# Attention in front of a routed mixture of experts: scores computed once per head in a corner of the array, the second softmax turned by VectorE

## The chip, the core and the metric

The kernel runs on one core of a Trainium2 chip. A core has TensorE (PE, matmuls from SBUF into the eight PSUM banks), VectorE (DVE), ScalarE (ACT), GpSimd (POOL, which does not read PSUM here) and SyncE (SP, which starts DMAs). Each engine works through its own queue in order and waits on semaphores for the others. The metric is the time of one execution on the device in microseconds; everything is float32.

## The reference

Eight batches of eight heads; a head has 512 tokens `x` and 32 state rows, each of 64 values. Tokens read the state and the state reads the tokens, from the same products with two different softmaxes; then every one of the 8 x 544 rows (512 values, all heads side by side) goes through one of eight experts.

```python
scores  = scale * x @ state.T                      # (B, H, 512, 32)
a       = softmax(scores);  xread = a @ state      # (B, H, 512, 64)
scores2 = scale * state @ x.T                      # (B, H, 32, 512): scores, transposed
a2      = softmax(scores2); sread = a2 @ x         # (B, H, 32, 64)
x       = concatenate([xread, sread], tokens)      # rows of H * D = 512 values
logits  = x @ w_gate;  local = sigmoid(x @ w_local)
# in token order: e = argmax(logits) where it is the first token or local < 0.5, else the e before
out     = softmax(logits)[e] * (relu(x @ w1[e]) @ w2[e])
```

## The kernel before

The program has three stages: `attention`, then `Routing.route`, then `experts`. The instructions of each engine are put in order by a scheduler of the framework, which places them by its own estimate, so the order in the code and that in the queues differ. Tiles rotate through pools; a tile of a pool with n buffers waits until the tile n before it has been read. All of PSUM is one pool of eight single banks (`bank()`).

**Attention** loops over the eight batches. `load` brings `x` twice: `x_t`, transposed (pairs of heads on 128 partitions, 512 tokens along them), and `x_n`, tokens on partitions; three buffers of each. At the start the state is laid out with zeros around it: `std` (its transpose, four heads on the diagonal of blocks, so that one 128x128 tile of weights serves two heads and two heads' rows are zero) and `sd` (the state itself, four heads a group on a block diagonal). `sw` is the product of the state with the gate weights (L121), so that a token's gate logits come from its softmax weights too.

For each of the two groups of four heads, `weights` computes the scores twice: `s2`, (head, state) on partitions over 512 tokens (L138), and `s1`, tokens on partitions over (head, state) (L144). From `s2` come the state's weights `e2` (max L148, Exp L152 with its sum, scaling L161), from `s1` the tokens' weights `e1` (max over 32 L155, subtraction L157, Exp L158, sum L163, multiplication on POOL L166). `turned` turns both by PE against an identity (L173, L178), with copies out of PSUM on ACT (L175) and DVE (L180). `read` multiplies: the state's reading `rps` (L188, copied to `rt` on DVE, L194), the tokens' values `v` (L201, copied to `xr` on ACT, L207), the tokens' logits (L204), and for the 32 state rows a transpose and their logits (L214, L217). Then the gate's softmax, and rows of 520 values (512 and 8 probabilities) go to `rows` in DRAM. The softmaxes of batch b + 1 are written ahead of `read` of batch b.

**Routing** starts with L288 on all tokens' logits: a chain of small DVE operations, transposes and matmuls that gives each token a slot, sorted by expert in blocks of 128. **Experts** runs 41 blocks, each with a gather of 128 rows (POOL), 4 MB of weights (SP), 4 transposes, 32 matmuls of 128 columns (L437), 8 of 512 (L442), and a scatter.

## Time and profile before

| what | value |
|---|---|
| runs (median of 3; lowest to highest) | 876.18 us; 876.18 to 879.81 |
| profiled execution, first to last instruction | 877.5 us (no other time is given for it) |
| PE busy, weight loads busy | 795.2 us (91%), 600.2 us (68%) |
| DVE, ACT, POOL busy | 182.8 us (21%), 111.1 us (13%), 103.5 us (12%) |
| attention, to the start of L288 | 179.9 us |
| routing, from L288 to the first gather | 179.9 to 216.9 us |
| experts | 216.9 us to the end |

The profiled execution's span lies among the runs' times, 1.3 us above their median. A line of the chain of waits reads: start in us, length in us, engine, tile, line of the kernel, number of records. A line of the groups reads: line, engine, operation, out<-in, shapes, count, then busy us and mean ns of one, then the engine's idle time before them and what ended it. A line of the stretches reads: from:to, length, then busy us (and count) of PE, of its weight loads, of DVE, ACT and POOL, then the granted clock of PE, the share of the DMA engines and GB/s.

### The profile page before, as it was taken

The page shows a single profiled execution, that of the slowest core. Times are in us where ns is not written, and L with a number is a line of the kernel's source. Part 1 is how long each engine was busy: PE and PEld are TensorE (multiplying, and loading weights), DVE is VectorE, ACT ScalarE, POOL GpSimd, SP SyncE. Part 2 cuts the span into 40 slices and gives each one's busy share as a digit, 9 for nine tenths or more (in the row PEclk, how much of TensorE's full clock was granted, in tenths as well). Part 3 has the DMA queues.
Part 4 walks back from the last instruction along what each step waited for, and adds up shares of the span by engine and source line. Part 5 has one row for each costly group of instructions (what it writes and reads, how often), then busy time and mean ns, then how long its engine had stood idle before and what let it go on. Part 6 is the DMA issues. An engine that isn't in the chain of part 4 may idle for free.

```text
span 877.5 us, 11051 instructions
## 1 busy us (share of the span) xinstructions
PE 795.2 (91%) x4658; PEld 600.2 (68%) x4658; DVE 182.8 (21%) x525; ACT 111.1 (13%) x200; POOL 103.5 (12%) x110
## 2 busy tenths in 40 slices
PE   6899999937899999999999999999999999999995
PEld 6588888927676666766757667576676766767663
DVE  2465555465100101001010010100101001001010
ACT  0333343310000010000100001000010000100000
POOL 2001110000110101101011010110100101001000
PEclk9799999965899999999999999999999999999998
DMA  8145531228488878888788788887888877788730
GB/s 335 49 148 177 198 118 55 102 87 354 155 318 301 297 286 304 321 297 300 277 306 317 292 296 292 307 316 281 297 298 303 316 287 290 292 307 308 271 144 1
DMA packets 25761, 219.41 MB, mean 250 GB/s; under 512 B 3760, under 2 KB 3760, under 8 KB 13168
## 3 DMA queue, kind: packets, MB, share of 16 engines
q1 hardware_dynamic: 14400, 189.29, 58.6%
q0 software_dynamic: 6560, 19.84, 6.0%
q10 hardware_dynamic: 4752, 9.58, 3.0%
q8 instruction: 37, 0.61, 0.3%
q14 instruction: 12, 0.10, 0.0%
HBM read 200.73 MB, written 19.80 MB: 251 GB/s over the span
## 4 chain that ended last, share of the span: by engine, by line
issue 65%; PE 21%; POOL 6%; DMA 4%; DVE 3%; POOLq 0%; SPq 0%; DVEq 0%
POOL out_dram L445 4%; PE ps L138 4%; PE ps L201 3%; PE ps L144 3%; PE ps L188 3%; DMA out_dram<-y,sidx 3%; PE ps L386 2%; POOL xg L401 2%; PE ps L121 2%; PE ps L204 1%; PE ps L178 1%; PE ps L173 1%; DMA sttc<-in_stt_dram 1%; DMA xg<-rows,gidx 0%; PE ps L214 0%
## 5 line engine op out<-in xcount | busy, mean ns | idle before, releaser
L437 PE MATMUL ps<-x_t,a 128*128 128x128 f32 x2624 | 305.9, 278 | 41.0 <-DVE x_t L430 41.0
L437 PEld LDWEIGHTS ps<-x_t,a 128*128 128x128 f32 x2624 | 298.1, 193 | 50.9 <-DVE x_t L430 50.9
L442 PE MATMUL ps<-c,h 128*128 128x512 f32 x656 | 288.3, 592 | 0.0
L442 PEld LDWEIGHTS ps<-c,h 128*128 128x128 f32 x656 | 121.5, 190 | 137.3 <-issue 137.3
L439 ACT ACTIVATE h<-ps 128x512 f32<-128x512 f32 x82 | 49.0, 597 | 632.5 <-PE ps L437 632.5
L401 POOL DMA_INDIRECT xg<-rows,gidx x41 | 40.0, 975 | 553.9 <-PE ps L428 500.0
L444 DVE TENSOR_SCALAR y<-ps,p 128x512 f32<-128x512 f32 x41 | 30.8, 751 | 284.6 <-PE ps L442 284.6
L423 DVE TENSOR_TENSOR own<-xg,ohb 128x8 f32<-128x8 f32 x41 | 6.9, 167 | 300.8 <-DMA xg<-rows,gidx 300.8
L445 POOL DMA_INDIRECT out_dram<-y,sidx x41 | 41.6, 1015 | 69.3 <-DVE y L444 58.0
L144 PEld LDWEIGHTS ps<-std,x_t 128*128 128x128 f32 x256 | 32.2, 197 | 8.8 <-issue 8.8
L428 PEld LDWEIGHTS ps<-ident,xg 128*128 128x128 f32 x164 | 20.7, 143 | 25.5 <-issue 25.5
L201 PE MATMUL ps<-sd,a 128*128 128x256 f32 x128 | 35.3, 398 | 0.0
L138 PE MATMUL ps<-x_t,std 128*128 128x512 f32 x64 | 33.7, 653 | 0.0
L166 POOL TENSOR_TENSOR e<-e,z 128x512 f32<-128x512 f32 x16 | 16.7, 1047 | 142.6 <-DVE z L160 109.6
L144 PE MATMUL ps<-std,x_t 128*128 128x128 f32 x256 | 32.0, 279 | 0.0
L188 PE MATMUL ps<-e,x_n 128*128 128x64 f32 x256 | 29.5, 273 | 0.0
L188 PEld LDWEIGHTS ps<-e,x_n 128*128 128x128 f32 x256 | 29.2, 192 | 0.0
L428 PE MATMUL ps<-ident,xg 128*128 128x128 f32 x164 | 25.1, 276 | 4.3 <-DMA xg<-rows,gidx 4.3
L430 DVE COPY x_t<-ps 128x512 f32<-128x512 f32 x41 | 27.9, 682 | 0.9 <-PE ps L428 0.9
L386 PE MATMUL ps<-bc,pc 128*128 128x41 f32 x80 | 17.3, 415 | 9.9 <-DVE bc L381 9.9
L386 PEld LDWEIGHTS ps<-bc,pc 128*128 128x128 f32 x80 | 17.1, 332 | 10.8 <-issue 10.8
L207 ACT COPY xr<-ps 128x512 f32<-128x512 f32 x32 | 18.8, 586 | 36.6 <-PE ps L201 36.6
(124 smaller groups left out, 343.1 us busy)
## 6 DMA issues: line engine op xcount, KB each, us to landing
a<-in_w_dram SPq DMA_DIRECT2D x41, 2048.0 KB, 7.8
c<-in_w_dram SPq DMA_DIRECT2D x41, 2048.0 KB, 8.9
rows<-xr ACTq DMA_DIRECT2D x8, 1040.0 KB, 4.3
x_t<-in_xt_dram SPq DMA_DIRECT2D x8, 1024.0 KB, 4.8
x_n<-in_xn_dram SPq DMA_DIRECT2D x8, 1024.0 KB, 5.4
xg<-rows,gidx POOLq DMA_INDIRECT x41, 8.4
out_dram<-y,sidx POOLq DMA_INDIRECT x41, 7.6
rows<-xs ACTq DMA_DIRECT2D x8, 65.0 KB, 4.0
```

Source lines behind the costliest of these rows:

```text
L138: nc.tensor.matmul(s2, lhsT=std[:, b, k, :], rhs=x_t[:, k, :], start=(k == 2 * g), stop=(k == 2 * g + 1))
L144: nc.tensor.matmul(s1[:, c * P:c * P + P], lhsT=x_t[:, k, c * P:c * P + P], rhs=std[:, b, k, :], start=(k == 2 * g), stop=(k == 2 * g + 1))
L188: nc.tensor.matmul(rps[:, k, :], lhsT=x_n[:, c, 2 * k:2 * k + 2, :].rearrange("p h d -> p (h d)"), rhs=e_t[k // 2][:, c, 64 * (k % 2):64 * ...
L201: nc.tensor.matmul(v[:, g * GD:g * GD + GD], lhsT=a_t[g][:, c * P:c * P + P], rhs=sd[:, b, g, :], start=True, stop=True)
L386: nc.tensor.matmul(who, lhsT=pc, rhs=bc[:, c], start=(c == 0), stop=(c == COLS - 1))
L401: nc.gpsimd.indirect_dma_start(out=xg, out_offset=None, in_=rows[:, :], in_offset=bass.IndirectOffsetOnAxis(ap=gidx[:, k:k + 1], axis=0))
L428: nc.tensor.transpose(tps[:, j * P:j * P + P], xg[:, j * P:j * P + P], ident)
L437: nc.tensor.matmul(hps[:, i * P:i * P + P], lhsT=a[:, j, m * P:m * P + P], rhs=x_t[:, j, :], start=(j == 0), stop=(j == KT - 1))
L439: nc.scalar.activation(h[:, half * 4:half * 4 + 4, :].rearrange("p m t -> p (m t)"), hps, Act.Relu)
L442: nc.tensor.matmul(yps, lhsT=h[:, m, :], rhs=c[:, m, :], start=(m == 0), stop=(m == FK - 1))
L444: nc.vector.tensor_scalar(y, yps, p, None, Alu.mult)
L445: nc.gpsimd.indirect_dma_start(out=out, out_offset=bass.IndirectOffsetOnAxis(ap=sidx[:, k:k + 1], axis=0), in_=y, in_offset=None, bounds_c ...
```

## The change

The scores are computed once. `scores` gives one head 64 rows and 32 columns of the array: pair k of heads goes to partitions 32k of the output, head u of the pair to bank u of a tile `s` of two banks (one buffer). All eight heads of a batch are one tile of 128 partitions and 2 x 512 columns. `softmaxes` then handles a batch at once, in operations of 1024 columns instead of two of 512: the state's weights `e2` from `s`, and the tokens' weights from `s` after DVE has transposed it in blocks of 32x32, so that 32 states lie along a row; POOL now subtracts the max as well as multiplying by the reciprocal, and a second 32x32 transposition by DVE makes `a`, the form that the products take. `turned` keeps the PE transposes of `e2` alone. The state with its gate logits is one tile `sd` of 256 + 9 columns a group; its logits come from `gates` in corners of the array too, and the separate logits product (L204) is gone: they come out of the value product and are added from its two groups by DVE. `std` and its layout are gone; `sd` is filled by POOL. PSUM in the attention is split: two single banks, two for `s`, two buffers of two banks for `v`; routing and experts have eight banks again. Rows get 530 values, their head order and that of `w1` differ to suit. The reductions, experts and routing are otherwise as they were, with later line numbers.

```diff
-XW = D + E
+VW = GD + E + 1
+XW = G * VW
...
+    sps = ctx.enter_context(tc.tile_pool(name="sps", bufs=1, space=PSUM))
+    vps = ctx.enter_context(tc.tile_pool(name="vps", bufs=2, space=PSUM))
...
+    def scores(b, x_t):
+        s = sps.tile([P, G, S], F32, name="s")
+        for k in range(KT):
+            for u in range(G):
+                r = slice(64 * u, 64 * u + 64)
+                nc.tensor.matmul(s[32 * k:32 * k + 32, u, :], lhsT=sttc[r, b, k, :], rhs=x_t[r, k, :],
+                                 start=True, stop=True)
+        return s
+
+    def gates():
+        for u in range(G):
+            w = bank()
+            r = slice(64 * u, 64 * u + 64)
+            for b in range(B):
+                for k in range(KT):
+                    nc.tensor.matmul(w[32 * k:32 * k + 32, b * (E + 1):(b + 1) * (E + 1)],
+                                     lhsT=sttc[r, b, k, :], rhs=wg[r, k, :], start=True, stop=True)
+            nc.vector.tensor_copy(sd[:, :, u, GD:], w[:, :B * (E + 1)].rearrange("p (b e) -> p b e", b=B))
...
-        nc.vector.tensor_reduce(nb, s2, axis=AX, op=Alu.max)
+        nc.vector.tensor_reduce(nb, s, axis=AX, op=Alu.max)
         nc.vector.tensor_scalar(nb, nb, -SCALE, None, Alu.mult)
...
+        nc.vector.transpose(e1f, s.rearrange("p g s -> p (g s)"))
...
+        for u in range(G):
+            nc.scalar.activation(e2[:, u], s[:, u], Act.Exp, bias=nb[:, u:u + 1], scale=SCALE,
+                                 accum_out=z2[:, u:u + 1])
...
+        nc.vector.tensor_reduce(m1.rearrange("p a o -> p (a o)"), e1, axis=AX, op=Alu.max)
+        nc.gpsimd.tensor_tensor(e1, e1, m1.to_broadcast([P, G * SC * 4, N]), op=Alu.subtract)
+        nc.scalar.activation(e1f, e1f, Act.Exp, scale=SCALE)
...
+        nc.gpsimd.tensor_tensor(e1, e1, z1.to_broadcast([P, G * SC * 4, N]), op=Alu.mult)
+        a = tp.tile([P, G, S], F32, name="a")
+        nc.vector.transpose(a.rearrange("p g s -> p (g s)"), e1f)
...
         for c in range(SC):
-            v = bank()
...
+            v = vps.tile([P, G, 512], F32, name="v")
+            for u in range(G):
+                nc.tensor.matmul(v[:, u, :VW], lhsT=a[:, u, c * P:c * P + P], rhs=sd[:, b, u, :],
+                                 start=True, stop=True)
+            nc.scalar.copy(xr[:, c], v[:, :, :VW])
+        nc.vector.tensor_tensor(lt[:, :SC, b, :], xr[:, :, 0, GD:], xr[:, :, 1, GD:], op=Alu.add)
...
+    s = scores(0, xs_[0][0])
+    gates()
+    soft = softmaxes(s)
     for b in range(B):
-        at = [turned(*s) for s in soft.pop(b)]
+        e = turned(soft[1])
+        a = soft[0]
         if b + 2 < B:
             xs_[b + 2] = load(b + 2)
         if b + 1 < B:
-            soft[b + 1] = [weights(b + 1, g, xs_[b + 1][0]) for g in range(G)]
-        read(b, [a for a, _ in at], [e for _, e in at], xs_.pop(b)[1])
+            soft = softmaxes(scores(b + 1, xs_[b + 1][0]))
+        read(b, a, e, xs_.pop(b)[1])
```

What this does to the queues is seen in a middle batch. On PE before, from the transposes of one batch through the scores of the next to its products:

```order
L173 MATMUL ps<-ident,e_296 128x128 x4
L178 MATMUL ps<-ident,e_301 128x128 x4
L173 MATMUL ps<-ident,e_327 128x128 x4
L178 MATMUL ps<-ident,e_332 128x128 x4
L138 MATMUL ps<-x_t,std 128x512 x2
L144 MATMUL ps<-std,x_t 128x128 x8
L138 MATMUL ps<-x_t,std 128x512 x2
L144 MATMUL ps<-std,x_t 128x128 x8
L188 MATMUL ps<-e,x_n 128x64 x16
L201 MATMUL ps<-sd,a 128x256 x2
L204 MATMUL ps<-sw,a 128x9 x2
```

On PE now, a whole round from one state product (L190) to the next (L131 the scores, L181 the transposes of e2, L203 the values with the logits, L212 and L215 the state's rows):

```order
L190 MATMUL ps<-e,x_n 128x64 x16
L131 MATMUL s<-x_t,sttc 32x512 x4
L212 MATMUL ps<-ident,rt 32x128 x4
L215 MATMUL ps<-wg,rt 32x9 x4
L131 MATMUL s<-x_t,sttc 32x512 x4
L181 MATMUL ps<-ident,e_740 128x128 x4
L203 MATMUL v<-sd,a 128x265 x4
L181 MATMUL ps<-ident,e_740 128x128 x4
L203 MATMUL v<-sd,a 128x265 x2
L190 MATMUL ps<-e,x_n 128x64 x16
```

The scores stand in two pieces around the state rows' transposes, and the value matmuls lie between other work instead of in one row behind the state product.

On ACT before, a round from the softmaxes of one batch to the rows sent off:

```order
L152 ACTIVATE e_462,z_463<-ps,nb 128x512
L158 ACTIVATE e_467<-e_467 128x512
L152 ACTIVATE e_493,z_494<-ps,nb 128x512
L158 ACTIVATE e_498<-e_498 128x512
L207 COPY xr<-ps 128x512 x4
L219 COPY xs<-ps 32x512
L175 COPY e<-ps 128x512
L226 ACTIVATE pr<-pr 128x40
L175 COPY e<-ps 128x512
```

And now (L157 the Exps of e2, L162 that of the tokens' weights, L205 the copies of v, L182 those of the turned e2):

```order
L157 ACTIVATE e_854,z_855<-s,nb 128x512 x2
L225 ACTIVATE pr<-pr 128x40
L162 ACTIVATE e_852<-e_852 128x1024
L205 COPY xr<-v 128x530
L232 DMA rows<-xr 128x4x530
L234 DMA rows<-xs 32x530
L205 COPY xr<-v 128x530 x2
L217 COPY xs<-ps 32x4x2x64
L182 COPY e<-ps 128x4x128
L205 COPY xr<-v 128x530
L182 COPY e<-ps 128x4x128
```

The copies of v, one row of four before, are now split, and the first of them stands behind the Exp L162, whose input comes from POOL's subtraction.

On DVE before, around the copies of the state product (L194):

```order
L157 TENSOR_TENSOR e_498<-ps,m_496 128x512
L165 RECIPROCAL z_473<-z_473 128x16
L160 RECIPROCAL z_494<-z_494 128x1
L194 COPY rt<-ps 64x128
L161 TENSOR_SCALAR e_493<-e_493,z_494 128x512
L163 TENSOR_REDUCE z_504<-e_498 128x16
L194 COPY rt<-ps 64x128
```

And now (L166 the scalings of e2, L168 the sum over the tokens' weights, L196 the copies to rt, L173 the second 32x32 transposition):

```order
L166 TENSOR_SCALAR e_740<-e_740,z_741 128x512 x2
L168 TENSOR_REDUCE z_752<-e_738 128x32
L196 COPY rt<-ps 64x128
L169 TENSOR_SCALAR z_752<-z_752 128x32
L196 COPY rt<-ps 64x128
L170 RECIPROCAL z_752<-z_752 128x32
L219 COPY lt<-ps 32x9
L148 TENSOR_REDUCE nb<-s 128x2
L173 STREAM_TRANSPOSE a<-e_738 128x1024
```

Both copies to rt now stand behind the sum L168, which waits for the Exp L162 on ACT; and the transposition that makes `a` comes after the next batch's max.

More of the change, by code (lines that the diff above doesn't have):

```diff
@@ new lines, in attention @@
+    sttc = once.tile([P, B, KT, N], F32, name="sttc")
+    nc.scalar.dma_start(out=sttc.rearrange("p b k n -> p (b k n)"), in_=stt)
+    xs_ = {0: load(0)}
+    stc = once.tile([P, B, G, DH], F32, name="stc")
+    nc.scalar.dma_start(out=stc.rearrange("p b g d -> p (b g d)"), in_=st)
+    xs_[1] = load(1)
+    sd = once.tile([P, B, G, VW], F32, name="sd")
+    nc.gpsimd.memset(sd, 0.0)
+    for j in range(4):
+        r = slice(32 * j, 32 * j + 32)
+        nc.gpsimd.tensor_copy(sd[r, :, :, 64 * j:64 * j + 64], stc[r])
@@ L427, in experts @@
         for j in range(KT):
-            nc.tensor.transpose(tps[:, j * P:j * P + P], xg[:, j * P:j * P + P], ident)
+            at = (j // 2) * VW + (j % 2) * P
+            nc.tensor.transpose(tps[:, j * P:j * P + P], xg[:, at:at + P], ident)
         x_t = hp.tile([P, KT, P], F32, name="x_t")
```

151 lines of the change are left out of this document (51 added, 100 removed).

## The prediction

> **What bounds the kernel now.** I read the page first: its 40 slices give the stages, about 22 us a slice.
>
> ```profile
> span 877.5 us, 11051 instructions
> PE   6899999937899999999999999999999999999995
> DVE  2465555465100101001010010100101001001010
> PEclk9799999965899999999999999999999999999998
> ```
>
> TensorE (PE) is full from the third slice to the end, except around slice 8. VectorE (DVE) works in the first eight slices alone, so these hold the attention and the routing, and all behind them is the experts, which the change leaves as they are. Then the busy times by stretch:
>
> ```profile
> 60.00:80.00 20.00, 20.00 (x143) 16.94 (x142) 11.43 (x37) 7.04 (x14) 2.09 (x2) 1.00 0.48 168
> 180.00:200.00 20.00, 4.67 (x19) 2.96 (x19) 16.45 (x48) 0.17 (x1) 0.00 (x0) 0.57 0.41 150
> 200.00:225.00 25.00, 19.88 (x92) 19.36 (x93) 11.94 (x44) 0.00 (x0) 3.99 (x4) 0.50 0.77 304
> ```
>
> Inside the attention (the first row) PE has no idle time, DVE is busy 11.4 of 20 us, ScalarE (ACT) 7.0, GpSimd (POOL) 2.1, and the DMA engines 48%. The routing (180 to 217 us) is a chain of DVE steps and small matmuls at half clock. So a batch of the attention costs what PE needs for it, and the chain of waits says what that is:
>
> ```profile
> 1.20 4.53 DMA sttc<-in_stt_dram
> ...
> 7.63 13.40 PE ps L121 x62
> 21.03 3.61 PE ps L138 x4
> ...
> 26.94 1.72 PE ps L138 x4
> ...
> 47.80 3.52 PE ps L188 x32
> ...
> 59.22 1.72 PE ps L138 x4
> 60.94 1.78 PE ps L144 x16
> ...
> 66.23 3.52 PE ps L188 x32
> 69.75 0.92 PE ps L201 x4
> 70.67 0.35 PE ps L204 x4
> 71.01 0.96 PE ps L201 x4
> ...
> 74.94 0.45 PE ps L214 x4
> 75.39 0.35 PE ps L217 x8
> 75.74 0.58 PE ps L173 x4
> 76.33 0.44 PE ps L178 x4
> ...
> 84.64 3.52 PE ps L188 x32
> ...
> 169.73 3.52 PE ps L188 x32
> ...
> 179.90 0.40 DVE eq L288
> ```
>
> Every piece of one batch is a PE piece. From L188 to L188 it is 84.64 - 66.23 = 18.41 us, and the pieces fill it: L188 3.52, L201 0.92 + 3 x 0.96 = 3.80, L204 4 x 0.35 = 1.40, L214 and L217 0.80, transposes 0.58 + 3 x 0.44 = 1.90, L138 2 x 1.72 = 3.44, L144 2 x 1.78 = 3.56; sum 18.42. A matmul in float32 shows as two records: the 512-column ones (L138, 4 records for 2 matmuls) cost 0.86 us each. The stage is then 47.8 (to the first L188) + 121.9 (seven steps, the last without new scores) + 10.2 (tail to L288) = 179.9 us. This sum is what the change moves.
>
> **The change on PE.** Per batch it removes L144 (3.56) and L204 (1.40) wholly, and half of the 16 transposes (0.90; the remaining eight cost 1.00 with the dearer first piece). L201 grows from 256 to 265 columns: 3.80 x 265/256 = 3.93. L188, L214, L217 stay. The scores become eight matmuls of 512 columns on 64 rows by 32 columns of the array, where four stood on all of it (3.44). That is the open price: no row of this trace has such a corner. If they run one after another, 8 x 0.86 = 6.88. If corners with different rows run side by side, the two records of one matmul still follow each other, because they use the same corner; only the second record of one matmul can lie beside the first of the next, which makes nine half-steps of 0.43, 3.87. If everything overlaps, about 0.9. I take 3.87, since neighbours in the order differ in their rows (u alternates inside k) and the records stay in order. PE per batch is then 3.87 + 1.00 + 3.52 + 3.93 + 0.80 = 13.1 us; serial it is 16.1, with all corners at once 10.2. PE also changes between corners and the whole array four to six times in a batch; the one change of shape in the rows, from 32 columns of weights to 128, made the first four transposes 0.58 instead of 0.44, so at most 0.8 a batch. I take nothing, because PE will have idle time beside it (below); without that it is the 0.8.
>
> **The other engines.** Prices from the groups:
>
> ```profile
> L148 DVE TENSOR_REDUCE nb<-ps 128x1 f32<-128x512 f32 x16 | 11.1, 692 | 24.5 <-PE ps L138 24.5
> L223 DVE TENSOR_REDUCE mx<-lt 128x5 f32<-128x40 f32 x8 | 1.6, 198 | 0.3
> L161 DVE TENSOR_SCALAR e<-e,z 128x512 f32<-128x512 f32 x16 | 8.1, 508 | 0.2
> L152 ACT ACTIVATE e<-ps,nb 128x512 f32<-128x512 f32 x16 | 11.0, 688 | 25.7 <-DVE nb L149 25.7
> L158 ACT ACTIVATE e<-e 128x512 f32<-128x512 f32 x16 | 10.1, 630 | 27.5 <-DVE e L157 27.5
> L226 ACT ACTIVATE pr<-pr 128x40 f32<-128x40 f32 x8 | 1.9, 239 | 0.4 <-DVE pr L225 0.4
> L207 ACT COPY xr<-ps 128x512 f32<-128x512 f32 x32 | 18.8, 586 | 36.6 <-PE ps L201 36.6
> L166 POOL TENSOR_TENSOR e<-e,z 128x512 f32<-128x512 f32 x16 | 16.7, 1047 | 142.6 <-DVE z L160 109.6 <-DVE z L165 16.7 <-PE ps L201 16.4
> L106 POOL MEMSET sd<- 128x4096 f32 x1 | 3.5, 3501 | 0.0
> masks.py:197 POOL MEMSET ident<- 128x128 f32 x1 | 0.2, 204 | 0.3 <-POOLq L469 0.3
> ```
>
> DVE: a reduce over 1024 is 692 + 512 x (692 - 198)/472 = 1.23 us, three of them 3.7. The 32x32 transposes (two of 1024) are not in the trace: between 1.0, at L161's pace, and 2.5, twice the reduce; I take the reduce's 1.23 each, the usual pace of one input. Two scalings make 1.0. The small ones are what today's 10.5 us a batch (11.43 x 18.4/20) leave beside ten 512-wide operations at 0.69 and the two scalings, 2.6, and with wider reciprocals and one more sum 3.1. DVE then needs 3.7 + 2.5 + 1.0 + 3.1 = 10.3 us, about as now. ACT: Exp over 1024 costs 630 + 512 x (630 - 239)/472 = 1.05; with two L152 forms, four v copies and two e copies about 7 us. POOL: the memset rows (204 ns at 128, 3501 at 4096) say that only 0.1 us is fixed, so a two-input operation over 1024 is 2.0 us (bounds 1.05 and 2.1), two per batch 4.0. No engine passes PE's 13.1 in sum.
>
> But the work of a batch is now one chain: max 1.23, nb 0.15, transpose 1.23, max 1.23, POOL subtract 2.0, Exp 1.05, sum 1.23, reciprocal 0.5, POOL multiply 2.0, transpose 1.23, together 11.9 us with a dozen hand-overs, near a step's length, and the queues are in order. Two waits come from it in each batch, by the rows of the order shown with the change. First, ACT: the v copies stand behind the Exp that waits for POOL's subtract, so after the second max a v copy lands 2.0 + 1.05 + 0.6 = 3.65 us later; PE has v matmuls for two buffers (2 x 0.98) and a group of transposes (0.5), so it waits 1.2. Second, DVE: the rt copies stand behind the sum over e (1.23) that waits for that Exp, and PE's next transposes (L212) wait for them, about 0.9 with the matmuls that lie between. Bounds of the two together: 0 (the next scores cover them) and 4.9 (3.65 + 1.23, nothing covers). I take 2.2, hence a step of 15.3 us.
>
> DVE's scalings also meet POOL now:
>
> ```profile
> 33.40 1.05 POOL L166 TENSOR_TENSOR e<-e,z 128x512 f32<-128x512 f32 x1 [27.59 <-DVE z L160]
> 33.79 0.94 DVE L161 TENSOR_SCALAR e<-e,z 128x512 f32<-128x512 f32 x1
> ```
>
> Beside POOL the 0.51 us scaling took 0.94. The cover is that DVE waits in that place for ACT's Exp anyway; without it, 0.4 to 0.9 us more in a batch.
>
> **Start and tail.** The std copies go, and sttc lands at 1.20 + 4.53 = 5.7. The gate matmuls become 64, 128 records with 32 columns of weights; L217's are 0.35/8 = 44 ns at full clock. L121's 62 records took 216 ns each against L204's 0.35/4 = 87, and all 13.4 us of them, so nine-column matmuls don't raise the clock; doubled, the gates cost 11.3 one after another, 5.6 overlapped, and I take 8.5, since neighbours there share their rows. The first scores at half clock take about 6 (3.61 against 1.72 in the rows above: double, till the clock rises), so the first max starts near 20 (now 24.6), and the first L190 (the old L188) follows 13 later, by the chain's first half, e's transposes and the next scores: 33.2 (now 47.8). By the Trainium skill, "TensorE: Matmul & The Clock Gate", Part 1, whatever follows the first 3.4 us of matmuls runs at full clock; the trace does not bear that out for L121, and by it the gates would take some 4 us less, the time 841. Tail: the last L190, five of eight v matmuls, L212 and L215, the copies: 3.5 + 2.5 + 0.8 + 1.9 = 8.7 (now 10.2).
>
> **The sum.** 33.2 + 7 x 15.3 + 8.7 = 149.0, against 179.9: 30.9 us less. The rows of x grow from 520 to 530 values, 2%, on DMA queues that are half idle in the attention; in the experts the gathers lie ahead of PE by two blocks. Costed at nothing. 877.5 - 30.9 = 846.6 for this execution's span; the runs' median, 876.18, lies 1.3 under it: 845.
>
> **Rivals.** Rival 2 needs the clock's fall after PE's pause at 31 us, in stretches of 1 us (PEclk is the third number from a row's end):
>
> ```profile
> 31.00:32.00 1.00, 0.00 (x0) 0.00 (x0) 1.00 (x5) 0.00 (x0) 0.00 (x0) 1.00 0.83 131
> 32.00:33.00 1.00, 0.00 (x0) 0.01 (x1) 1.00 (x5) 0.48 (x1) 0.00 (x0) 0.71 0.84 344
> 33.00:34.00 1.00, 0.98 (x4) 0.71 (x4) 1.00 (x5) 0.15 (x1) 0.60 (x1) 0.50 0.95 401
> ```
>
> 1. The corners run one after another. Then it doesn't do what it says on PE: 16.1 + 1.5 of waits = 17.6 a step; gates 11.3 and first scores 11 put the first L190 at 43: 43 + 123.2 + 8.7 = 174.9, 5 us less, 871. For it: no row shows two matmuls at once; against it: nothing in the trace either, only that the two corners of a pair share neither rows nor PSUM bank.
> 2. Slower, by the clock. PEclk went from 1.00 to 0.50 inside the third idle microsecond, and L121 shows that a queue full of thin matmuls doesn't count as work. If serial scores on an eighth of the array count as idle, they run at half clock: 13.8 + 9.2 = 23 a step, 43 + 161 + 9 = 213, 33 us more: 909. It decides as soon as such matmuls fill most of a clock window; over 18.4 us a step it loses. Against it: the other 9 us of each step are full matmuls.
> 3. All corners at once, 0.9 us a batch, PE 10.2. Then the chain of 11.9 plus hand-overs sets a step of about 13.3: 24 + 93 + 9 = 126, 54 less: 822. For it: eight different corners; against it: two records of one corner stand next to each other. The Trainium skill, "TensorE: Matmul & The Clock Gate", Part 3 ("Measured speedup vs the span model"), says that packed tiles start about 4 ns apart and the whole takes one matmul and these 4 ns each. No run here shows it yet.
> 4. Right on PE, but the chain is longer: transposes at 2.5 us. It adds 2.5 to a step, of which PE's waits absorb 0.9: 33.2 + 7 x 16.9 + 9 = 160.5: 857.
>
> **Chances.** Forecast 0.50, its own range 836 to 854 (waits 1.0 to 3.5, gates 5.6 to 11.3); rival 1 0.25; rival 2 0.08; rival 3 0.07; rival 4 0.10. The range 826 to 873 leaves out rivals 2 and 3 and the upper edge of 1. A measurement of this kernel tells 0.5% from no change, about 4.4 us: under 871.8 is faster. Rival 1 lies on that edge (0.13 faster, 0.10 same, 0.02 slower), so faster 0.80, same 0.10, slower 0.10.
>
> **What would show it.** The scores' group (L131, 128 records): 8 matmuls in 3.9 us of the chain means right, 6.9 rival 1, about 1 rival 3. STREAM_TRANSPOSE near 1.23 and POOL's two lines near 2.0. A distance from L190 to L190 of 15.3 in the chain, with PE idle 2 us of it for ACT's xr copies (L205) and DVE's rt (L196). L290 near 149. From there to the end the same 698 us as now; if that part moves, the argument is wrong in a place that I have not priced. Granted clock near 1.0 between 60 and 140; 0.5 there is rival 2.

## The result, and the profile after

The changed kernel takes 835.23 us (median of 4; 834.05 to 836.63) against 877.4 us for the kernel before on the same chip: a ratio of 0.951, interval 0.9488 to 0.9532. The forecast was 845 us with a range of 826 to 873; the time lies just under the forecast's own, narrower range, 836 to 854. One run of one experiment below (riding undone on the changed kernel, 853.14 us) fell in the chip's slow state and is left out of that kernel's figures. The profiled execution of the changed kernel took 836.63 us. Its page has, for the lines shown of before:

```profile
span 834.8 us, 10290 instructions
...
PE   3987986579999999999999999999999999999995
...
DVE  4656873820100100100100110010010010010010
...
PEclk9988997559999999999999999999999999999998
```

PE now has gaps in the first seven slices, where it was full. The chain of waits (start, duration, what) gives the marks of the stage:

```profile
1.21 6.85 DMA x_t<-in_xt_dram
8.11 2.04 PE s L131 x16
10.17 1.23 DVE nb L148
...
14.34 1.28 ACT L157
15.64 1.46 ACT e L157 x4
17.14 1.91 PE s L131 x2
...
53.94 6.47 PE ps L190 x32
...
89.37 1.75 DVE pr L224
...
115.53 1.92 DVE pr L224
...
137.41 0.40 DVE eq L290
```

The attention ends at 137.41, where it ended at 179.90 and the forecast had 149.0. From there to the end it is 834.8 - 137.41 = 697.4 us; before it was 877.5 - 179.9 = 697.6. So all of the gain, 42.5 us, is in the attention, and the start of L290 (or the line that stands for it) is a mark that some of the experiments below are compared by.

PE's timeline from 22 us names the first read product, and the stretches say what lies on either side of it (length, then busy time of PE, weight load, DVE, ACT and POOL; third from the end the granted clock):

```profile
22.76 1.43 PE L190 MATMUL ps<-e,x_n 128*128 128x64 f32 x6
```

```profile
0.00:22.80 22.80, 9.41 (x169) 3.93 (x169) 8.94 (x21) 4.96 (x8) 11.53 (x19) 1.00 0.90 368
22.80:128.50 105.70, 92.15 (x583) 67.22 (x579) 73.67 (x159) 46.36 (x92) 29.18 (x21) 0.89 0.43 156
128.50:137.40 8.90, 7.57 (x55) 6.51 (x53) 2.26 (x13) 2.40 (x5) 0.00 (x0) 0.93 0.36 131
54.00:71.00 17.00, 16.31 (x84) 12.56 (x84) 6.93 (x17) 6.34 (x12) 3.17 (x3) 0.70 0.45 155
90.20:101.00 10.80, 10.26 (x82) 7.57 (x80) 8.64 (x20) 5.81 (x11) 2.92 (x4) 1.00 0.58 205
```

The first L190 starts at 22.76 instead of 47.8: 25.0 us of the 42.5. Seven steps take 105.7 instead of 121.9 (15.1 each, 13.2 of it with PE busy): 16.2 us. The tail takes 8.9 instead of 10.2: 1.3 us. The steps are uneven, from 10.8 us (the last row) to 17.0 and 19.2. The groups and PE's waits up to 138 us:

```profile
L203 PE MATMUL v<-sd,a 128*128 128x265 f32 x128 | 40.6, 461 | 6.0 <-DVE a L173 4.8 <-ACT xr L205 1.1
L131 PE MATMUL s<-x_t,sttc 64*32 64x512 f32 x128 | 20.6, 715 | 9.2 <-ACT e L157 7.2 <-DMA x_t<-in_xt_dram 2.0
L161 POOL TENSOR_TENSOR e<-e,m 128x1024 f32<-128x1024 f32 x8 | 15.3, 1913 | 31.4 <-DVE m L160 18.7 <-DVE lt L206 5.4 <-DVE z L169 4.8
L153 DVE STREAM_TRANSPOSE e<-s 128x1024 f32<-128x1024 f32 x8 | 9.9, 1238 | 0.0
L224 DVE TENSOR_TENSOR pr<-lt,mx 128x40 f32<-128x40 f32 x8 | 7.6, 952 | 0.2
L141 PE MATMUL ps<-wg,sttc 64*32 64x9 f32 x128 | 1.8, 199 | 4.3 <-DMA sttc<-in_stt_dram 4.3
```

```profile
PE s L131 <- ACT e L157: 7.2, 2, 7.1
PE v L203 <- DVE a L173: 4.8, 2, 4.0
...
PE ps L190 <- ACT e L182: 4.1, 2, 3.4
...
PE ps L212 <- DVE rt L196: 1.9, 2, 1.4
...
PE v L203 <- ACT xr L205: 1.1, 2, 0.7
```

A line of the waits reads: who waited, for what, us in total, how often, the longest.

The gates (L141) take 1.8 us where L121 took 13.4. The scores (L131) take 20.6 us in all, and their mean of 715 ns hides how they come. PE's timeline (x counts records, two to a matmul; three places):

```profile
33.96 1.04 PE L131 MATMUL s<-x_t,sttc 64*32 64x512 f32 x2
37.05 1.08 PE L131 MATMUL s<-x_t,sttc 64*32 64x512 f32 x12
...
74.77 1.09 PE L131 MATMUL s<-x_t,sttc 64*32 64x512 f32 x16
```

One matmul takes 1.04 us, six take 1.08, all eight 1.09. All corners run at once; what costs is a *piece*, a group of them with other matmuls before and behind it. The scheduler left 17 pieces for the eight batches.

### The profile page after: what moved, and what is told of

Its sections match the earlier page's. It is cut to its first block, busy times and chain, and to the rows that moved or that the text cites. A ratio compares the mean times of both kernels' runs of the same rounds, so it can differ in the third digit from the quotient of the medians.

```text
span 834.8 us, 10290 instructions
## 1 busy us (share of the span) xinstructions
PE 736.5 (88%) x4338; PEld 534.0 (64%) x4338; DVE 177.2 (21%) x442; ACT 102.9 (12%) x187; POOL 122.5 (15%) x122
## 4 chain that ended last, share of the span: by engine, by line
issue 68%; PE 10%; DVE 8%; POOL 7%; DMA 4%; ACT 1%; POOLq 0%; SPq 0%; ACTq 0%
POOL out_dram L448 4%; DMA out_dram<-y,sidx 3%; PE v L203 3%; PE ps L388 2%; POOL xg L403 2%; PE s L131 2%; PE ps L190 2%; DVE nb L148 1%; DVE pr L224 1%; DVE e L153 1%; DMA x_t<-in_xt_dram 1%; PE ps L181 1%; DVE z L168 1%; DVE a L173 1%; DVE m L160 1%
## 5 line engine op out<-in xcount | busy, mean ns | idle before, releaser
L203 PE MATMUL v<-sd,a 128*128 128x265 f32 x128 | 40.6, 461 | 6.0 <-DVE a L173 4.8
L190 PEld LDWEIGHTS ps<-e,x_n 128*128 128x128 f32 x256 | 33.3, 212 | 7.0 <-ACT e L182 5.0
L203 PEld LDWEIGHTS v<-sd,a 128*128 128x128 f32 x128 | 26.8, 224 | 17.2 <-DVE a L173 6.6
L190 PE MATMUL ps<-e,x_n 128*128 128x64 f32 x256 | 33.7, 296 | 4.1 <-ACT e L182 4.1
L131 PE MATMUL s<-x_t,sttc 64*32 64x512 f32 x128 | 20.6, 715 | 9.2 <-ACT e L157 7.2
L388 PEld LDWEIGHTS ps<-bc,pc 128*128 128x128 f32 x80 | 17.1, 332 | 10.8 <-DVE bc L383 10.8
L205 ACT COPY xr<-v 128x530 f32<-128x530 f32 x32 | 18.8, 599 | 31.8 <-PE v L203 30.4
L161 POOL TENSOR_TENSOR e<-e,m 128x1024 f32<-128x1024 f32 x8 | 15.3, 1913 | 31.4 <-DVE m L160 18.7
L171 POOL TENSOR_TENSOR e<-e,z 128x1024 f32<-128x1024 f32 x8 | 15.3, 1912 | 30.7 <-DVE z L170 20.7
```

The costliest lines, as they stand in the source:

```text
L131: nc.tensor.matmul(s[32 * k:32 * k + 32, u, :], lhsT=sttc[r, b, k, :], rhs=x_t[r, k, :], start=True, stop=True)
L190: nc.tensor.matmul(rps[:, k], lhsT=x_n[:, c, 2 * k:2 * k + 2, :].rearrange("p h d -> p (h d)"), rhs=e[:, c, :, 32 * k:32 * k + 32], start= ...
L203: nc.tensor.matmul(v[:, u, :VW], lhsT=a[:, u, c * P:c * P + P], rhs=sd[:, b, u, :], start=True, stop=True)
L388: nc.tensor.matmul(who, lhsT=pc, rhs=bc[:, c], start=(c == 0), stop=(c == COLS - 1))
```

## Experiments

Every kernel was timed in three rounds beside the kernel before. The scheduler draws up the queues anew for each kernel, so a difference of 4 us, and more, between two kernels can be their order (see the run with scores twice); where the order stayed, the text says so. In the kernels with scores in one or six pieces, lines from L132 on stand one number higher than in the changed kernel (L132 is L131; L150, L154, L162, L172, L183, L191, L204, L225 are L149, L153, L161, L171, L182, L190, L203, L224). In the two runs on the kernel before they stand higher too: L123 is its L121, L142 and L148 are its L138 and L144, and the read product L188 is L190 in the first run and L192 in the second.

**Gates in corners, alone.** On the kernel before:

```diff
-                nc.tensor.matmul(wps[:, i:i + E + 1], lhsT=std[:, b, k, :], rhs=wg[:, k, :],
-                                 start=(k == 2 * g), stop=(k == 2 * g + 1))
+                for u in range(2):
+                    r, j = slice(64 * u, 64 * u + 64), 2 * (k % 2) + u
+                    nc.tensor.matmul(wps[32 * j:32 * j + 32, i:i + E + 1], lhsT=sttc[r, b, k, :],
+                                     rhs=wg[r, k, :], start=True, stop=True)
```

> The kernel before (877), with one part of the change alone: the state's gate logits (its L121) as 128 matmuls of one head each, straight from the loaded state, in the 64x32 corners, instead of 32 matmuls with the zero-padded weights; scores, transposes and the rest as before. Theory (the larger part of the gain, 25 us, lies ahead of the first read product, and 11.6 us of it in the gates, which took 13.4 us and take 1.8 in corners, on PE's queue ahead of the first scores): the attention of the kernel before starts 8 to 13 us earlier, 864 to 869. Rival (the start is set by the copies into the padded weights or by the loads): 874 to 878.

Measured: 865.35 us, ratio 0.9855 (0.9826 to 0.9884). PE's timeline has the gates and the first read product:

```profile
5.86 1.90 PE L123 MATMUL ps<-wg,sttc 64*32 64x9 f32 x128 [5.86 <-DMA sttc<-in_stt_dram]
...
34.58 3.68 PE L190 MATMUL ps<-e,x_n 128*128 128x64 f32 x32
```

The first read product moves from 47.64 to 34.58, 13.1 us, and every step stays at 18.42. The theory holds: the gates alone are 13.1 of the 25.0 us at the start, since the zero-padded weights (their copies ended at 6.75) and 13.4 us of nine-column matmuls at half speed stood ahead of the first scores.

**Row scores in corners too.** The same kernel, with `s2` (L138 of the kernel before), which feeds the state's weights and not, as the expectation says, the token softmax:

```diff
-            nc.tensor.matmul(s2, lhsT=std[:, b, k, :], rhs=x_t[:, k, :],
-                             start=(k == 2 * g), stop=(k == 2 * g + 1))
+            for u in range(2):
+                r, j = slice(64 * u, 64 * u + 64), 2 * (k % 2) + u
+                nc.tensor.matmul(s2[32 * j:32 * j + 32, :], lhsT=sttc[r, b, k, :], rhs=x_t[r, k, :],
+                                 start=True, stop=True)
```

> The kernel with only the gates in corners (865.35), with one part more of the change: of the two score orientations, which both stay, the one of the token softmax (its L140, two 128x128 matmuls a group, 1.88 us warm) as four 64x32 corner matmuls a group. PE's order stays as it was, and its steps of 18.42 us have no idle time on PE, so that what PE saves is what the step loses. Theory (four corners run side by side in about 1.06 us, the two records of each matmul included): 0.8 us a group, 1.6 to 1.7 us a batch, steps of 16.8, 11 to 15 us below 865. Rival (the two records of one corner hold up the next corner, as my prediction had it: about five half steps of 0.52, 2.6 us a group): 0.7 us a group more, 0 to 13 us above 865.

Measured: 855.23 us, ratio 0.9743 (0.9719 to 0.9767), 10.1 us below, just under what the theory had. Some 4.6 us of it lie ahead of the first read product, which starts at 29.95 instead of 34.58. PE's timeline in a step, with the order as before:

```profile
58.82 1.06 PE L142 MATMUL ps<-x_t,sttc 64*32 64x512 f32 x8
59.81 2.05 PE L148 MATMUL ps<-std,x_t 128*128 128x128 f32 x16
61.79 1.06 PE L142 MATMUL ps<-x_t,sttc 64*32 64x512 f32 x8
62.78 2.05 PE L148 MATMUL ps<-std,x_t 128*128 128x128 f32 x16
64.67 3.68 PE L192 MATMUL ps<-e,x_n 128*128 128x64 f32 x32
```

Four corners take 1.06 us of records and 0.99 us of PE, where the two full matmuls took 1.72: the corners run side by side, and the rival falls. But the piece behind, between two visits to the corners, now takes 61.79 - 59.81 = 1.98 where it took 1.78; the second one, with a product on the whole array behind it, takes 64.67 - 62.78 = 1.89. So each change between corners and whole array costs 0.1 us, whichever way it goes, and a visit with its return 0.2. A group then saves 0.73 - 0.20 and a step 1.06: 18.42 - 1.06 = 17.36, which is what the read products show (47.31 to 64.67).

**Scores twice.** On the changed kernel, `for u in range(G):` became `for u in (0, 1, 0, 1):` in `scores`.

> The changed kernel with each of the 64 score matmuls of L131 issued a second time into the same corner of the same bank, so that PE does 16 of them a batch instead of 8 and nothing else is added. Theory (all eight corners run side by side, a piece of up to eight such matmuls takes about 1.05 us whatever their order, and PE is busy for some 12.7 us of a 15.1 us step): about 1.05 us of PE more a batch, 8.4 us in all, of which the idle time takes up a part: 2 to 9 us above the changed kernel's 835, L131 going from 20.6 to about 29 us busy. Rival 1 (pairs of one corner run one after the other, as my prediction had it, 3.87 us a batch): 3.9 us more a batch, 25 to 31 us above. Rival 2 (PE has room, the chain of softmaxes sets the step): within 2 us of the changed kernel.

Measured: 831.61 us, ratio 0.9457 (0.9426 to 0.9487): 3.6 us *below* the changed kernel, outside all three expectations. On the price of corners it is clear all the same: L131 was 30.0 us busy, as the theory had, and PE's timeline shows 15 matmuls in one piece of 1.98 us:

```profile
110.33 1.98 PE L131 MATMUL s<-x_t,sttc 64*32 64x512 f32 x30
```

So two matmuls of the same corner follow each other, and eight corners stand beside each other. That 9.4 us more of PE's work came out faster means that the order drawn up for this kernel was worth more: L203 took 37.4 us instead of 40.6, L190 30.3 instead of 33.7, and PE waited 1.1 us instead of 4.1 for L182, 0.2 instead of 6.0 ahead of L203, but 5.6 instead of 1.9 for L196.

**One piece, six pieces.** The same instructions as the changed kernel, with the scores written ahead in the scheduler's eyes:

```diff
+        with tc_.high_priority(offset=200):      # 30 in the run with six pieces
             for k in range(KT):
```

> The changed kernel with the scheduler told to put the eight score matmuls of a batch next to each other; in the changed kernel they stand on PE in one to three pieces a batch (17 pieces over eight batches: 1 and 7, or 1, 1 and 6, or 4 and 4, with other matmuls between), here in 8 pieces of eight. The same instructions. The order of the other work moves with it, since the scheduler draws it up anew. Theory (PE pays about 1.0 us for a piece of scores, however many of the corners are in it): about 9 us of PE saved, 3 to 9 us below the changed kernel's 835. Rival (a piece costs by its count): within 2 us of it, but for what the other order does.

> As the run with one piece, but with a smaller head start for the scores, by which the scheduler puts them in mostly six pieces a batch (1, 1, 1, 1, 1, 3), with a transpose, a 9-column product or a value product between them. The same instructions. Theory (1.0 us a piece): some 48 pieces against 17, 30 us of PE more, of which the idle time takes up at most 2 us a batch: 14 to 30 us above the changed kernel's 835, and L131 busy 45 to 50 us instead of 20.6. Rival (a piece costs by its count): L131 stays near 21 us and the time within 4 us of the changed kernel.

Measured: one piece 820.29 us, ratio 0.9334 (0.9308 to 0.936); six pieces 846.19 us, ratio 0.9643 (0.9615 to 0.967). The scores' group in the two:

```profile
L132 PE MATMUL s<-x_t,sttc 64*32 64x512 f32 x128 | 11.3, 772 | 12.8 <-ACT e L158 10.8 <-DMA x_t<-in_xt_dram 2.0
```

```profile
L132 PE MATMUL s<-x_t,sttc 64*32 64x512 f32 x128 | 43.6, 715 | 9.0 <-ACT e L158 7.1 <-DMA x_t<-in_xt_dram 2.0
```

The same 128 records are 11.3, 20.6 or 43.6 us of PE, in 8, 17 or 40 pieces: about 1.05 us for each, and 1.9 to 2.0 for each of the first two or three, while PE still ran at half speed (in the kernel with one piece those at 8.26, 17.49 and 29.04). On PE the theory holds (9.3 us saved for "about 9", 43.6 for "45 to 50"); in time it misses both ways. One piece gave 14.9 us where 3 to 9 were expected; beside the scores its value products (L204) took 6.5 us less, 34.1 instead of 40.6. Six pieces cost 11 us by the medians, not 14 to 30, and their runs spread (840.30 to 848.49): the traced execution is the fastest of them, and its attention ends at 140.74, only 3.3 us after the changed kernel's. There the 23 us more of scores were given back in two parts: PE waited 4.6 us in the seven steps instead of 13.6, and ran at full speed, its value products in 33.5 us instead of 40.6, its read products (L191) in 29.8 instead of 33.7. What the other executions lose besides, no trace shows. The stretch of seven steps, one piece and then six:

```profile
22.00:112.90 90.90, 79.55 (x576) 61.61 (x576) 76.60 (x157) 44.67 (x90) 28.97 (x21) 1.00 0.50 182
```

```profile
21.80:132.40 110.60, 105.99 (x578) 63.16 (x579) 71.31 (x157) 44.81 (x91) 29.20 (x21) 1.00 0.44 151
```

With six pieces PE is busy 106 of 110.6 us: there PE nearly alone sets the step (15.8). With one, a step is 13.0 us with 11.4 on PE.

**The riding of the logits, undone.** On the one-piece kernel, and on the changed kernel:

```diff
-                nc.tensor.matmul(v[:, u, :VW], lhsT=a[:, u, c * P:c * P + P], rhs=sd[:, b, u, :], ...
-            nc.scalar.copy(xr[:, c], v[:, :, :VW])
-        nc.vector.tensor_tensor(lt[:, :SC, b, :], xr[:, :, 0, GD:], xr[:, :, 1, GD:], op=Alu.add)
+                nc.tensor.matmul(v[:, u, :GD], lhsT=a[:, u, c * P:c * P + P], rhs=sd[:, b, u, :GD], ...
+            for u in range(G):
+                nc.tensor.matmul(lps[:, c * (E + 1):(c + 1) * (E + 1)], lhsT=a[:, u, c * P:c * P + P],
+                                 rhs=sd[:, b, u, GD:], start=(u == 0), stop=(u == G - 1))
+            nc.scalar.copy(xr[:, c, :, :GD], v[:, :, :GD])
+        nc.vector.tensor_copy(lt[:, :SC, b, :], lps[:, :SC * (E + 1)].rearrange("p (c e) -> p c e", c=SC))
```

> The kernel with the scores in one piece (820), with the riding of the logits undone: value products of 256 columns, the logits as 8 matmuls of 9 columns a batch into a bank of their own, xr copied without its gate columns (these filled with zeros by POOL). Theory (a step of 12.9 us has PE busy for about 11.5 us of it, so PE's work counts nearly in full): the 9-column records add 16 x 0.05 to 0.06 us a batch and the value products lose 9 of 265 columns, 0.4 to 0.8 us a batch: 2 to 7 us above 820. Rival (the products have room, and the copy of the logits from a bank frees DVE from adding two SBUF inputs): within 2 us, or below.

> The changed kernel (835) with the riding of the logits undone as in the run before on the one-piece kernel, where it cost 22.5 us: its 9-column matmuls were 19.0 us busy on PE, 266 ns a matmul of two records. Theory (these records cost PE 2.0 to 2.4 us a batch whatever the order, as L204's 236 ns in the kernel before): 12 to 24 us above 835. Rival (the 22.5 us were the order of that one kernel and its pauses of the clock): within 6 us of 835.

Measured: on one piece 842.83 us, ratio 0.9619 (0.9566 to 0.9672), 22.5 us above it; on the changed kernel 839.25, 839.60 and 845.55 us, ratio 0.9589 (0.9536 to 0.9642), 4 to 10 us above it. PE's timeline of the first (L206 the values, L209 the logits), at full speed and, later, at half speed after two waits:

```profile
62.79 0.51 PE L209 MATMUL ps<-sd,a 128*128 128x9 f32 x4
63.15 1.11 PE L206 MATMUL v<-sd,a 128*128 128x256 f32 x4
...
71.97 5.78 PE L191 MATMUL ps<-e,x_n 128*128 128x64 f32 x32 [1.60 <-ACT e L183]
...
104.17 7.09 PE L191 MATMUL ps<-e,x_n 128*128 128x64 f32 x32 [3.93 <-ACT e L183]
```

From start to start a nine-column record costs 0.36/4 = 0.09 us, as L204 did before (0.35/4), and not the 0.05 to 0.06 of my first expectation: 1.4 us a batch, 11.5 in all, less about 1 us for the 9 columns that the value products lose. That is the part of riding which belongs to PE. The 22.5 us have a wait of 3.93 us in them that the one-piece kernel did not have, after which the read product ran at half speed (7.09 against 3.8) as did what followed it up to 121; before that, after a wait of only 1.60 us, the read product at 71.97 took 5.78 and PE was slow up to 83. On the changed kernel the traced execution's attention ends at 140.52, 3.1 us later than without the edit, and the time lies mostly under PE's part, since the order was drawn anew there too. The first expectation is met on neither side. Of the second, the theory's 12 to 24 us are not met, and the rival's 6 us hold for two runs of three. Riding is worth some 10 us on PE by these rows; in time it was 4 to 10 us in one kernel and 22.5 in the other, by what the order made of it.

**The gate softmax without its maximum.** On the changed kernel:

```diff
-        nc.vector.tensor_tensor(pr, lb, mx[:, :, b:b + 1].to_broadcast([P, NC, E]), op=Alu.subtract)
-        nc.scalar.activation(pr, pr, Act.Exp)
+        nc.scalar.activation(pr, lb, Act.Exp)
```

> The changed kernel without the subtraction of the largest logit in the gate softmax (L224 left out, Exp taken of the logits themselves; mathematically the same probabilities). L224 is the instruction of two SBUF inputs that took 0.95 us in the mean here, up to 1.91, where it ended together with a POOL multiplication or subtraction, against 0.2 us in the kernel before. Theory (L224 waits for POOL and stands on the chain with 6.9 us of the first 138): 3 to 7 us below the changed kernel's 835. Rival (the wait lies beside PE's work and only moves to the next instruction, L163, L227 or L230): within 2 us of it.

Measured: 831.34 us, ratio 0.9455 (0.9425 to 0.9485), 3.9 us below. It lies in the theory's range, but L163 rose from 494 to 688 ns (the stall moved there in part, as the rival had it), and an order drawn anew gave 3.6 us by itself in the run with scores twice. It decides little.

**POOL and DVE.** Two runs on the one-piece kernel. In the first both POOL instructions of the state softmax go to DVE (`nc.gpsimd.tensor_tensor(e1, ...)` to `nc.vector.tensor_tensor(e1, ...)`, twice); in the second the negated maximum goes to ACT (`nc.scalar.mul(nb, nb, -SCALE)`).

> The kernel with the scores in one piece (820), with the subtraction (L162) and the multiplication (L172) of the state softmax on DVE instead of POOL, so that POOL runs nothing beside DVE. In that kernel's steps two small DVE instructions a batch, L150 (128x2) and L225 (128x40), take 1.7 us each and end with POOL's instruction. Theory (they are held up by POOL's use of the same path to SBUF): they fall to 0.2 us, 3 us less a batch, against two instructions of about 1.2 us more on DVE, while the chain loses 0.7 us at each: 2 to 10 us below 820. Rival (DVE, about 10 us busy without the stalls, becomes the bound when it takes 2.4 us more in a step of 12.9): 0 to 10 us above 820.

> The kernel with the scores in one piece (820), with L150 (the negated and scaled maximum, 128x2) on ACT instead of DVE. On DVE it took 1.05 us in the mean, 1.7 in the middle steps, ending with POOL's multiplication, and the transposition L154 and all behind it waited. Theory (the stall belongs to the kind of DVE instruction, and a transposition out of PSUM runs beside POOL): L154 starts about 1.4 us earlier in the middle steps, 3 to 9 us below 820. Rival (the transposition, or the next instruction, waits for POOL's end just so): within 2 us.

Measured: 819.88 us, ratio 0.9337 (0.9308 to 0.9367), and 820.16 us, ratio 0.9347 (0.9317 to 0.9377): both the same as the one-piece kernel's 820.29. In the first the stalls are gone: L225 fell from 940 to 197 ns in the mean and L150 from 1049 to 246, while the two moved instructions take 1.22 us each on DVE; by these sums the new work took what the stalls gave. In the second L150's stall went, and L164's mean rose from 270 to 594 ns: the next instruction of the kind took its place, and the attention of the traced execution ended 2.4 us earlier (119.39 against 121.75), which the runs' medians do not show.

So the third takes one of each: the negated maximum on ACT, and only the subtraction L162 on DVE.

> The kernel with the scores in one piece (820), with both L150 on ACT and the max subtraction L162 on DVE, so that POOL runs one multiplication a batch and neither of the two small DVE instructions stands beside it. DVE gains 1.22 us and loses about 1.5 (L225) and 1.05 (L150) a batch. Theory (DVE has the room that it had not when both POOL instructions came to it, and the stalls go): 2 to 8 us below 820. Rival (PE's 11.5 us set the step, the stalls lie beside it): within 2 us.

Measured: 815.17 us, ratio 0.9287 (0.9258 to 0.9317), 5.1 us below one piece, as the theory had, and the fastest of all: 20 us below the changed kernel. L225 is at 195 ns, L164 at 162. The attention ends at 115.17, 6.6 us earlier than with one piece:

```profile
19.80:106.80 87.00, 79.95 (x578) 63.23 (x579) 70.69 (x157) 45.14 (x98) 15.68 (x14) 0.92 0.54 202
```

Seven steps take 87.0 us with PE busy 80.0 of them: 12.4 a step, 11.4 on PE, 3.9 us less than in the kernel with one piece. Another 2.2 us lie ahead of the steps and have a cause that the expectation did not name: with L150 on ACT, ACT loads its table (1.28 us) at 1.69, while it has nothing else to do, and not at 14.70 with the first Exp waiting behind it; the first read product starts at 19.82 instead of 22.02. So not all of the 5.1 us are stalls, and with the order drawn anew the share of the stalls stays open. The granted clock of 0.92 shows what is left: the read product at 32.50 took 5.38 us for 24 of its 32 records, at half speed, after waits of 1.21 and 0.73 us.

**Without the second transposition.** On the one-piece kernel, `nc.vector.transpose(a..., e1f)` is left out and the value products read e1 itself.

> The kernel with the scores in one piece (820) without the second VectorE transposition (L174): the value products read the state softmax as it lies after POOL's multiplication, so their values are others, their shapes the same. It takes 1.24 us a batch from DVE and from the chain to the value products. Theory (PE, some 11.5 us busy in a step of 12 to 13, sets the step): the chain gives back little, 0 to 6 us below 820. Rival (the chain over DVE and POOL sets the step): 1.2 us a batch, 8 to 10 us below, and PE idle less by as much.

Measured: 817.98 us, ratio 0.9307 (0.9279 to 0.9334), 2.3 us below: the theory's side, less than a new order can give, and short of the rival's 8 to 10. DVE gave back little of its 10 us, for the scaling L167 now stood beside POOL (788 ns in the mean instead of 483).

## Why the prediction was right, and where not

**Right: what bounds, and where it ends.** The gain lies in the attention alone, the rest is 697.4 against 697.6 us. PE's work still makes up most of a step. In total the step came out at 15.1 (forecast 15.3), with 13.2 on PE and 1.9 of waiting (13.1 and 2.2); the tail at 8.9 (8.7).

**Right sizes by luck: the waits.** The forecast's 2.2 us of waiting a step were to come from ACT's copies xr (L205, 1.2) and DVE's copies rt (L196, 0.9). The waits above have 1.1 and 1.9 us for these in all eight batches together, 0.4 us a batch. Most of the rest are two long waits that the forecast did not have: 4.0 us for `a` (L173) and 3.4 us for the turned `e2` (L182), each in one batch. In the first, L173 stood on DVE behind L224 and L163, which took 1.55 and 1.91 us there beside POOL's instructions; in the second, the copy L182 stood on ACT behind the gate's Exp L225, which waited for DVE's L224. That these add up to what was forecast is chance.

**Mis-sized: the gates and the first scores.** The error of the forecast, 149.0 against 137.41, is 11.6 us, and 10.4 of it is the start: the first L190 at 22.76 instead of 33.2. The term "I take 8.5, since neighbours there share their rows" was 1.78, and "the first scores at half clock take about 6" was 2.0; so the first max started at 10.17 instead of near 20 (sttc also came 1.4 us earlier than in the kernel before, and the scores then waited 2.0 us for x_t, which the forecast left out). Both terms rest on one idea, that two records which share rows or a corner hold up the next corner. The trace has no sign of it. The way from the first max to the first L190 was 12.6 us, as forecast (13): inside it the second scores waited for the first batch's Exp (7.1 us in the waits above), which came behind 1.28 us in which ACT loaded its table (14.34 in the chain). The start of rival 1, 43, is 41 by the terms named for it; nothing hangs on it.

**Wrong reason, right step: the scores.** 3.87 us a batch were forecast ("the second record of one matmul can lie beside the first of the next, which makes nine half-steps of 0.43"). By the prediction's own sign ("about 1 rival 3") rival 3 was right here: all eight corners take 1.09 us. That PE's 13.2 us nonetheless fit is luck, and has two causes that rival 3 did not have either. The scores came in up to three pieces, at 1.0 us each: 2.1 us a step (14.85 in the seven, by L131's own share of that stretch). And PE ran part of the time at half speed: the granted clock, forecast near 1.0, was 0.89 over the seven steps. Where PE had waited 3.35 us for L182 the read product took 6.47 us (3.7 elsewhere), and where it had waited 4.0 us for L173 the next twelve records of L203 took 5.64 (1.96 for eight elsewhere); over all batches L203 cost 40.6 us, against 34.1 in the one-piece kernel, which has no such wait in its middle steps and a granted clock of 1.00 in them.

The Trainium skill, "TensorE: Matmul & The Clock Gate", Part 1, puts PE at half clock after an idle window of about 3.4 us, and at full clock after about 3.4 us of sustained matmuls. (By that rule the prediction's gates, 8.5 us, would lose 2.6 us, an estimate, and not the 4 that it gave.) The waits of 3.35 and 4.0 us agree with the first half, but so long a wait was not needed: the changed kernel's granted clock fell once more at 123 us, after no wait above 1.39 us, and that of the kernel before within a wait of 2.6 us (the prediction's rows from 31 to 34). The second half the rows do not bear out: after the 3.35 us PE had no pause, and the granted clock still read 0.50 from 55 to 64 us; and the nine-column matmuls of the kernel before ran 13.4 us without a pause at half speed. What brings the clock up or down, these runs leave open.

The run with one piece shows what the forecast's own picture would have been worth with rival 3's scores: 13.0 a step, near rival 3's 13.3, and 820 us, near its 822. That nearness is not rival 3's mechanism, though. It had the chain set the step with PE busy 10.2 of it; PE was busy 11.4 of the 13.0, and the run without the second transposition, 1.24 us of the chain, gave 2.3 us in all and not 8 to 10.

**Rival 3's rule.** One matmul of two records took 1.04 us, eight of sixteen 1.09: 0.05/7, some 7 ns for each further matmul. The Trainium skill, "TensorE: Matmul & The Clock Gate", Part 3, "Measured speedup vs the span model", gives one matmul and about 4 ns for each further tile. Inside a piece the runs agree with the form of that rule, and have 7 ns in place of its 4 for these float32 matmuls.

**Mode changes: costed at nothing, measured at 0.1 us for each change, 0.2 for a visit to the corners and back.** In the kernel with row scores in corners, without idle time, they showed in full. That the changed kernel's waits cover them, as the forecast had it, no run shows.

**DVE beside POOL: right kind, wrong place.** The forecast expected it at the scalings L166. In the changed kernel those never met POOL (476 ns), and it was L224 and L163 that did. The timelines of three kernels, POOL's row and the DVE row that ends with it; first the changed kernel, then the one-piece kernel, then the changed kernel with riding undone:

```profile
89.14 1.91 POOL L161 TENSOR_TENSOR e<-e,m 128x1024 f32<-128x1024 f32 x1 [5.37 <-DVE lt L206]
...
89.37 1.74 DVE L224 TENSOR_TENSOR pr<-lt,mx 128x40 f32<-128x40 f32 x1
```

```profile
57.51 1.91 POOL L172 TENSOR_TENSOR e<-e,z 128x1024 f32<-128x1024 f32 x1 [7.40 <-DVE z L171]
57.72 1.73 DVE L150 TENSOR_SCALAR nb<-nb 128x2 f32<-128x2 f32 x1
```

```profile
87.83 1.91 POOL L161 TENSOR_TENSOR e<-e,m 128x1024 f32<-128x1024 f32 x1 [2.62 <-DVE z L163]
...
88.45 1.97 DVE L166 TENSOR_SCALAR e<-e,z 128x512 f32<-128x512 f32 x2
```

An instruction of 40 or of 2 elements a partition ends only when POOL's 1024 are done. Which one is hit depends on the order, and taking one away hands the wait to the next (L164 in the run with the maximum on ACT).

**The other prices.** Transposes 1.24 us (forecast 1.23, rival 4's 2.5 falls), POOL 1.91 (2.0), reduces 1.20 to 1.22 (1.23), Exp over 1024 1.05.

**Where the 42.5 us come from**, as far as the runs part it: gates 12.1 us (877.4 to 865.35), row scores in corners 10.1 (to 855.23), the rest 20.0 (to 835.23): the other orientation of the scores, eight PE transposes, the softmaxes a batch at a time, and the riding. These are not parted further than by the 4 to 10 us of riding above, and the sum has the accidents of each kernel's order in it.

## What to carry to other kernels

Packed corner matmuls cost by the piece, not by the matmul: put all that belong together next to each other on PE's queue, and look in the timeline whether the scheduler kept them so. Price the thin matmuls of a prologue by their own rows: here they ran at half speed with everything queued behind them. When an instruction is held up beside another engine's, moving work can move the wait: both POOL instructions moved gave nothing, one moved together with the smallest DVE instruction gave 5 us, 2 of them by an earlier table load on ACT. And when a total comes out as forecast, check its terms: here the waits and the scores had other causes than those that were summed.

## What the runs showed of the hardware

- 128 records of nine columns on 64x32 corners took 1.78 to 1.90 us, 14 to 15 ns each; on the whole array such a record takes 90 ns from start to start, and took 216 in the first 20 us of the kernel before and 209 at 111.05 in the one-piece kernel with riding undone, where the granted clock reads 0.50.
- Two 64x32 matmuls on the same corner follow each other (1.98 us for 15 matmuls), eight on different corners stand beside each other though each is two records (1.09 us).
- A change between 64x32 corners and the whole array: 0.1 us each way (1.98 and 1.89 against 1.78 us for the same sixteen records).
- After waits of 3.35, 3.93 and 4.0 us PE ran at half speed for several us, and also after one of 1.60 us (71.97 in the one-piece kernel with riding undone). The granted clock does not always show half speed: in the one-piece kernel the first L191, at 22.02, took 7.09 us, as long as the one at 104.17 with riding undone, in a stretch whose granted clock reads 1.00.
- DVE instructions with two inputs in SBUF, and single-input scalings from SBUF to SBUF of 2 to 512 elements, ended only with the POOL instruction beside them or after it (0.15 or 0.2 us become up to 1.9); one scaling of a single element, at 48.45 in the kernel before, did not wait. Reductions and 32x32 transposes in the same place did not stretch (1.25 us at most, one of them at 53.06 in the changed kernel beside POOL's 53.24 to 55.15). The Trainium skill, "GPSIMD Engine Reference", 1. Specifications, says that the two engines share SBUF interfaces, with contention for instructions in a two-port mode or with two SBUF inputs. The rows with two SBUF inputs agree, and in them the wait lasts until POOL's instruction ends; whether the scalings run in a two-port mode no row shows.
